# State-space convolution and feed-forward gradients on one core: the magnitudes of the next half block are loaded ahead of the current half block's stores, in a newly laid-out order

## The chip, the cores and the metric

One core of a Trainium2 chip runs the kernel. The metric is the device time of one execution in microseconds (us). Three runs of the kernel before took 584.26, 578.71 and 573.95 us, with a median of 578.71 us. The profile is of one further execution that took 580.12 us.

## The reference

The kernel computes a gated block and all its gradients. The input x (2048 x 512, bf16) is normalised row by row; the normalised rows xn go two ways. One is a long convolution per channel, whose 2048-tap kernel K is made from a diagonal state-space model (512 channels, 128 states each); the other is a feed-forward layer of width 1792. The gate multiplies them.

```python
dt = jnp.exp(log_dt)[:, None]
logdA = dt * (A_re + 1j * A_im)
P = jnp.exp(logdA[:, :, None] * jnp.arange(L)[None, None, :])
K = jnp.einsum("dn,dnl,dn->dl", C_re + 1j * C_im, P, dt * (B_re + 1j * B_im)).real
...
s = irfft(rfft(K padded) * rfft(xn padded))[:L] + xn * Dskip
g = silu(silu(xn @ w1) @ w2)
out = x + s * g
# and the gradients of all inputs for a given grad_out
```

The powers P are what the change concerns. The power exp(logdA * e) has a magnitude exp(dt * A_re * e) and a phase dt * A_im * e. The kernel doesn't make all 2048 of them: it makes 30 per channel and state, and products of these give the rest.

## The kernel before

The 512 channels are worked in four blocks b of 128, and each block in two half blocks h of 64 channels, so there are eight half blocks, (0,0) to (3,1). The work is written as Python generators; each `yield` ends a step. Strings of letters, PLAN, say which generator takes its next step, one letter a step, in seven stages. Each engine (TensorE is PE, VectorE is DVE, ScalarE is ACT, GpSimd is POOL, SyncE is SP, which issues most DMAs) executes its own instructions strictly in the order in which the strings make them, and waits for others by semaphores. SLOTS names the buffer of each tile, and WAYS says for each copy out of PSUM, in the order of its stream, whether ACT (A) or DVE (D) does it. All three were laid out ahead of time by a planner; the kernel only plays them.

Stage 1 (letters F, X, J, P, Q, R, C, U, 9) is where the change lies. In it, `gen_magnitudes` of the setup has already written the 30 magnitudes of all half blocks to Md in DRAM, 128 x 1920 bf16 a half block (480 KB). Then, for each half block:

- P, `gen_phases`: DVE makes the phases V (two tiles, L577 and L580), ACT the sine and cosine sn (L584).
- Q, `gen_powers`: SP loads the magnitudes into one fixed region of the tile ds, columns 5376 to 7296 (L597). DVE multiplies sn by them (L611): one instruction for the first 15 exponents (128x1920) and three for the last 15 (128x640, 128x896, 128x384). They write E, columns 0 to 2688 of ds, the first eighth of Y, and H. SP stores E to Ed (L613). DVE makes the rest of Y in two rounds of three instructions (m1, m2, Y: L622, L624, L626), and SP stores Y to Yd (L628).
- R, `gen_kernel_rows`: DVE multiplies E by the output weights into W (L646), PE contracts W with Y (L652), and after both half blocks of b the rows KE go through DMAs into Kb (L684).
- C, `gen_conv_fwd`: the forward transform of Kb, its product with the spectrum of xn (L477 to L485 on DVE), and the inverse transform.

There is one magnitude region and one E region for all eight half blocks. So the next half block's first multiply needs three things: its magnitudes have landed; the store of the last E has left; all W that read the last E are made. In the kernel before, the load of the magnitudes is the first step of a half block's Q, and so stands on SP behind the Ed and Yd stores of the half block ahead.

X and U are the transforms of xn, F is the feed-forward layer on PE (L764, L781), with J turning its rows. The stages after it hold the backward transforms (D, B), the feed-forward gradients (A, x, w, v) and the gradients of the state-space weights (V, T, S, Z).

Of the kernel before, what the change touches and what calls it, by code (L numbers as in the profile page):

```python
# [24 lines left out]


PLAN = """
2211p22355561566370476p666714575673676601p77167577307777JJ767F85370F7777577p77667763F778677064F88367F7F6FFF8437F67FFFF46
3F66F67FJ67J6F48877F86F68F73/FXXXXJXXFXXFPPFPFQFJPPXFFFPFPFFQFFFFX9QFFPUFFUQXFQXJXFQQQXQPXQXRFFJRPPPRRFXQRFFXPRFQXXRRFPQ
QQFXFFRRFXQQXFFFFFFQQRQFFRFXFUQQQXRRPJPFFXXPRXRFRPFRFXRRFFUPRRFJRRPFRQPRRRRQRQQXXXFXQRRRFQXQQCXRFQPRFQRXPFXFRFQFPFCPRRRU  # L30
FPCCFCCRFCRCQRCCXQFCQQCCPFFCQXQCFRQXFFQQQCCRPFCRCRRCCPFQPXRRRFFCFCFCFRCRRQFXXFRQRXCXQCXQXFFFXRQRCQCQFCRCRRFQCFFRPQCQFFJC
FQPCFRRCXRPRXRPFCCXRXRRPPCPXRCRFUJXXFPXRQXQCQRQPFCFQFXFCQXQRCCQFCFCFCQFFCPCRFFRFFFRFCCFPFCRFCCCQJCCRRRCFRQCCCPRRXCFCCXQC
CXRXQXFQCPRQPFXRJFQCCXRCQPCQRXRCCQFRCCFCRQRQXQRXRRFRFPCFRXPXRUFRCPRFXCCRFFRXFFFQFFXFXRCFQCRCCCCFJFQRXCCQQCFCJFRRQQQRCCCQ
RCCRQRRUCCCRFRRCRCRCRCRRCCRFCRRRRCCR/GGGCFCCGFCGCGFCCFCCGFFFCCCCGCFFCCCCGFLGCCFFGFGGCCCCFFGGFHGFGCCCCCGWCCHFFGHGCFCCGGFC
GCFCCFCCCCGCWFCHCCWCHWWCWHCCWMDHGWCWDGWCWHCCWWWDCDWDDWWGDDWWWWWWDWDLMDWDDMDLCWWLLMDDM/DDDddaDsDDdEaEDADsoaWodBAAABAABADA
DoBADAABDAaBABlDBADABoAADBsDAOBBAAABAOBDaDAABoBABBBABDBDBDBxBBsBADEoxBBBdOoBABOlABxBoxOdoBoxODBAlDBOlOAooxOBaDBBAOEODsxB
DBDDBxOBxaOxDsBBxBBBAOodoBBABADoBoADABBBoBBDBBABDAoBDABdAABDEOAABBxBBAaAABAADDsAooaBBAdBDAAOBBDlBBAOOBlABAAABsDdODDxDDAB
DODoDABODAxADEoDxoOsoAOBDxABBoaBBBAOdxaBOxBoBAABAOoDBOADOABADBDOABxDBBdAxBOBBDBoDxBBsDxEDoBDAoOABBBBaBABBDAABxxDBABABssB
EOOBOBBxBABBxaBBAxBxaABBBBAAaOAABBABBAAOBxBBBAAAAsdAxBBBxBdsBxABBBABBABBABBBsABA/NAYYNNANAYNNVxxddAVAaxYVVAVVYAAVVVYAYVT
AxVVTVATATxVVAATAAAVVVNTxsNTAANAxAVTAATTAVTNSVAVAVYVxNxVYxTYxSYVSTTTYVVATVVxSY/VVTVhVVTVVhttTtVVYTTTSVVYtTVwShtTYVStVVVT  # L40
TVwtTVVwStTtVwTVVZtVVTZtTYVVSSZTTVYVgtwTNNTwYNwgYNVYTShYVvZYVYVvZTVYvVTShYtNVTVtVVTVvvYTwTVtVTgZVVTwSVtVTTvTvSgVtTVvVVtT
TTwVVtTYZVtYhVTVVZVTwwhwVVVZVSTvSNVZTTwZVvTvNYTSNNwYTVtVZtvvtSZtTZYttTvZYYtSVVvhVSTVvVTTTVVVwYYZVTTvtVVVTVTSZTtSwZtTYwVY
VVVwhVVVYSVVSVTVYZTZwtVgVgTTTtwTVVZtZTwvTVYtVZSTZTYVtYShVTVZhwTwSvZZvVYvZZYtVTVvTVZTSTVvtZTvVgTVVVtTTwTgZSTTvSTZvZtZZStS
wZtvZZghvwtZvtZhhZtwwtwZgvZZwZvtZwwZtvv/iitvtkktkwtkvkiimvktwmkkmkvgvmvkmvkwvmkktwvvmkmgkitgwkvvikkmwkkvmmvikvtkvmmvktvg
kwkkwimmvvkmkwvvvkmmvkvvmkvmvkvvvmmvmvm
""".replace("\n", "").split("/")


SLOTS = dict(x.split("=") for x in """
fp.XT=01010101;pf.pf=012012012012012021021020120120121210210210210210210120102102120120121021021021021201201201201201021  # L50
021021021020102102101012012010120210212120101201212102102102102102101021212012010210121210121012012012021021021201202012
0120121012102102102102102;fp.hT=0101010101010101;dft.w8=21301203120131231032102321302310;pc.pc=0101010101010110101010101
010101010101010101010101010101010101010100110101010101010101010101010101010101010101010101010101010101010110101010101010
101011010101010101010101010101010101010101010101010101011010101010101010101010010101010100101001101010101010101010101010
1;fp.ob=0101010;tbl.tv=01011101110101011010101010101010;tbl.ts=01010101010111010010101011010010;tbl.W=010101101011010110
10;dft.t4=010011010101;gate.g=30127456;gate.S=01;da.doT=01010101;da.dhT8=20120120;dftb.w8b=1010;da.dhT6=10101010;go.go_s
=01010101;go.go_r=010101;go.go_g=01010101;go.go_x=01201201;da.pd_s=010101010101;sb.YT=2012012012012012;sb.Eb=01010101;sb
.Gb=01010101;sb.Vb=0101010101010101;sb.Tp=0101010101010101;sb.Sa=1010;fw.h_in=01201201201201;fw.a_tok=10101010101010;fw.
o11=01201201201201;sb.g_acc=0101;fw.dh_tok=0120120;fw.o10=1010101;lw.pd_l=012301;lw.Gt=01230123;lw.m=010101;lw.o1=120312
03  # L60
""".replace("\n", "").split(";") if x)

WAYS = """J=DADAADAA;
F=DDAAAAAAAAADDAAAAAADAAAAAAAAAAAAAAAAAAAAAAADADDAAAAAAAAAAAADDAADDDDADAAA;
X=AAAAAAAAAAAAAAAAAAAAAAAAAAAAAADA;
U=AD;
R=DDAAAAAAAAAAAAAAAAADAADADAADDAAAAAAADDDAAADAAAAA;
C=DDDAAAAAAAAAAAAAAAAADDAAAAAAAADAAAAAADAADAADAADAADDDDDADAAAAAAAA;  # L70
W=ADDDDDDDDDDDDD;
D=AAAADDAAAAAAAAADAAAAAAAAAADAAAAAAAAAAADA;
d=DDDDDAAD;
B=AAAAAAAAAADAAAAAAAAAAAAAAAAAADADADAAAADAAAAAAAAAAAAADADD;
x=ADAADAADAADA;
V=AAAAAAAAAADAAAAADDAAAAAAAAAAAAAAAAADAAADDAAAAAAAAAAAAAAAAAAAAAAA;
Y=DAAAAAAA;
w=AAADAAAAAAAAAA;
v=ADADDADAAAAAADAAAAAAAAAAAAAA"""
# [509 lines left out]
def gen_powers(k, b, h):  # L589

    nc, tbl = k.nc, k.tbl
    TT = nc.vector.tensor_tensor
# [4 lines left out]
    nc.sync.dma_start(tab[:, 5376:5376 + 64 * NX], k.Md[2 * b + h])  # L597
# [4 lines left out]
    k.E[b, h] = E
    for x0 in (0, 15):
        sn = k.sn.pop((b, h, x0))
        if x0 == 0:
            parts = ((E[:, :, :, 1:16, :], 0, 15),)
        else:
            parts = ((E[:, :, :, 16:NE, :], 0, 5), (Y[:, :, :, 1:8, :], 5, 12), (H, 12, 15))
        for o, i0, i1 in parts:
# [1 line left out]
            TT(out=eq(o), in0=qe(sn[:, i0:i1]), in1=qe(m), op=ALU.mult)  # L611
        yield
    nc.sync.dma_start(k.Ed[b, h], tab[:, 0:2688])  # L613
# [4 lines left out]
    out = lambda c: Y[:, c, :, 8:32, :].rearrange("p q (k m) a -> p q k m a", m=8)
    for c, (x, y), op in ((0, ((0, 0), (1, 1)), ALU.subtract), (1, ((0, 1), (1, 0)), ALU.add)):
        m1 = tbl.tile(shp, BF16, name="m1", tag="tv", bufs=2)  # L620
        m2 = tbl.tile(shp, BF16, name="m2", tag="ts", bufs=2)
        TT(out=m1[:], in0=lo(x[0]), in1=hi(x[1]), op=ALU.mult)  # L622
        yield
        TT(out=m2[:], in0=lo(y[0]), in1=hi(y[1]), op=ALU.mult)  # L624
        yield
        TT(out=out(c), in0=m1[:], in1=m2[:], op=op)  # L626
        yield
    nc.sync.dma_start(k.Yd[b, h], Y[:].rearrange("p c q j a -> p (c q j a)"))  # L628
    yield
# [847 lines left out]
```

## Time and profile before

| what | value |
|---|---|
| median of three runs | 578.71 us (573.95 to 584.26) |
| the profiled execution | 580.12 us, span of its instructions 578.3 us |
| PE busy | 527.0 us, 91% of the span |
| DVE busy | 523.8 us, 91% |
| ACT busy | 445.8 us, 77% |
| POOL busy | 77.7 us, 13% |
| moved by DMA | 144.49 MB, 250 GB/s over the span |

The span runs from the first to the last instruction; the 1.8 us between it and the execution's time lie around it. A busy share is an average over stages: PE and DVE have the same share of the span, though not in the same stages. "Idle before" is the time that an engine stood still just ahead of an instruction, and the releaser is what ended it. The chain of waits is followed back from the last instruction, at each step to what released it; a step on it needn't be one that the engine stood still for. Two rows of the page belong to the DMAs that the change moves: the eight loads of magnitudes took 6.8 us each from issue to landing (median), the eight stores of E 6.1 us.

### The profile page before, as it was taken

The numbers are of one execution on the slowest core, as the hardware profiler recorded it, in microseconds if no ns is written. First come the engines' busy times: TensorE is split into PE (matmuls) and PEld (weight loads), VectorE is DVE, ScalarE is ACT, GpSimd is POOL, SyncE is SP. The second block draws the span as 40 slices with busy tenths as digits, with TensorE's granted clock in tenths as the row PEclk, the third lists the DMA queues.
The fourth block names the chain that finished last, engine by engine and source line by source line (L and its number), as shares of the span: only waits on it lengthen the run. The fifth ranks groups of instructions, "written<-read, shape, count | busy, mean of one in ns | idle before, by whom it ended". The sixth has DMA issues, their size and how long they took to land.

```text
span 578.3 us, 14484 instructions
## 1 busy us (share of the span) xinstructions
PE 527.0 (91%) x5982; PEld 395.3 (68%) x6008; DVE 523.8 (91%) x823; ACT 445.8 (77%) x555; POOL 77.7 (13%) x164
## 2 busy tenths in 40 slices
...
GB/s 264 313 276 193 196 281 238 319 260 250 325 225 227 337 287 328 295 254 251 318 261 276 314 249 247 210 208 189 270 231 214 192 272 219 220 199 264 198 204 120
DMA packets 156643, 144.49 MB, mean 250 GB/s; under 512 B 83488, under 2 KB 132896, under 8 KB 153504
## 3 DMA queue, kind: packets, MB, share of 16 engines
...
q0 software_dynamic: 6640, 19.67, 10.1%
...
HBM read 62.78 MB, written 59.25 MB: 211 GB/s over the span
## 4 chain that ended last, share of the span: by engine, by line
PE 41%; DVE 18%; DMA 13%; issue 12%; ACT 9%; POOL 4%; SPq 3%; POOLq 0%; ACTq 0%; DVEq 0%
PE ps_da L1169 8%; PE ps_dx L1193 7%; DMA ds<-Md 6%; PE ps_w L1232 5%; PE ps_i L451 3%; PE ps_v L1021 3%; ACT dA L116 2%; PE ps_w L1261 2%; PE ps_i L464 2%; PE psS L1058 2%; PE pt_t L138 2%; DVE ds L611 2%; DMA YD<-Od 2%; SPq L495 2%; PE ps_s L406 1%
## 5 line engine op out<-in xcount | busy, mean ns | idle before, releaser
L116 ACT CAST dA<-ps_s 128x1024 bf16<-128x1024 f32 x85 | 85.1, 1033 | 9.0 <-PE ps_s L406 6.3
L116 ACT CAST Vb<-ps_v 128x672 bf16<-128x672 f32 x58 | 41.2, 732 | 35.5 <-PE ps_v L1021 23.6
L764 PE MATMUL ps_h<-XT,W 128*128 128x256 bf16 x448 | 57.5, 281 | 10.8 <-DVE XT L117 8.9
L764 PEld LDWEIGHTS <-W 128*128 128x128 bf16 x448 | 43.7, 101 | 19.0 <-issue 11.7
L1169 PE MATMUL ps_da<-doT,W 128*128 128x256 bf16 x448 | 56.2, 273 | 0.0
L1261 PE MATMUL ps_w<-dh_tok,xn 128*128 128x256 bf16 x448 | 52.0, 273 | 2.1 <-ACT o L116 2.0
L116 ACT CAST dB<-ps_i 128x1024 bf16<-128x1024 f32 x42 | 41.6, 1029 | 12.4 <-PE ps_i L451 12.4
L1193 PE MATMUL ps_dx<-W,dhT 128*128 128x512 bf16 x224 | 51.0, 379 | 0.0
L781 PE MATMUL ps_o<-W,aT 128*128 128x512 bf16 x212 | 49.4, 379 | 1.6 <-ACT aT L772 0.6
L1232 PE MATMUL ps_w<-YD,a_tok 128*128 128x512 bf16 x210 | 49.2, 379 | 0.7
L1261 PEld LDWEIGHTS <-xn 128*128 128x128 bf16 x448 | 43.2, 98 | 7.9 <-issue 2.8
L1172 DVE TENSOR_TENSOR dhT<-ps_da,dhT 128x512 bf16<-128x512 f32 x56 | 37.8, 684 | 10.1 <-PE ps_da L1169 9.4
L1169 PEld LDWEIGHTS <-W 128*128 128x128 bf16 x448 | 41.5, 98 | 7.6 <-issue 1.4
L781 PEld LDWEIGHTS <-aT 128*128 128x128 bf16 x224 | 21.1, 98 | 26.2 <-ACT aT L772 2.2
L1193 PEld LDWEIGHTS <-dhT 128*128 128x128 bf16 x224 | 21.1, 98 | 24.2 <-issue 1.2
L1232 PEld LDWEIGHTS <-a_tok 128*128 128x128 bf16 x224 | 21.4, 98 | 23.6 <-ACT a_tok L1223 0.7
L1223 ACT ACTIVATE a_tok<-pt_t 128x1024 bf16<-128x1024 bf16 x28 | 29.1, 1042 | 3.2 <-PE pt_t L138 3.2
L584 ACT ACTIVATE sn<-V 128x1920 bf16<-128x1920 int16 x16 | 29.4, 1835 | 2.5 <-DVE V L580 1.6
L1021 PE MATMUL ps_v<-Gb,YT 128*128 128x168 bf16 x256 | 26.8, 238 | 4.7 <-DMA YT<-Yd 2.2
L1038 DVE TENSOR_TENSOR Tp<-Vb,Eb 128x1344 bf16<-128x1344 bf16 x32 | 27.2, 852 | 3.4 <-ACT Vb L116 3.3
L406 PEld LDWEIGHTS <-TF 128*128 128x128 bf16 x384 | 24.9, 100 | 7.9 <-issue 4.8
L477 DVE TENSOR_TENSOR cm<-sp_in,dA 128x2048 bf16<-128x2048 bf16 x24 | 29.3, 1219 | 0.8
(244 smaller groups left out, 1236.9 us busy)
## 6 DMA issues: line engine op xcount, KB each, us to landing
Yd<-YD SPq DMA_DIRECT2D x8, 1024.0 KB, 6.3
sp_in<-Ud SPq DMA_DIRECT2D x8, 1024.0 KB, 6.3
...
Ed<-ds SPq DMA_DIRECT2D x8, 672.0 KB, 6.1
Eb<-Ed SPq DMA_DIRECT2D x8, 672.0 KB, 4.9
...
KXd<-dA SPq DMA_DIRECT2D x4, 1024.0 KB, 5.7
```

Source lines behind the costliest of these rows:

```text
L116: return self.nc.scalar.copy(out=out, in_=in_)
L406: nc.tensor.matmul(out=ps[:, j], lhsT=k.TF[:, 8 * h + j, c, :], rhs=U(8 * h + j), start=True, stop=True)
L477: TT(out=t2[:], in0=b[:, :, gs], in1=a[:, 1:2, gs].to_broadcast([P, 2, n, P]), op=ALU.mult)
L584: nc.scalar.activation(out=sn[:, 0:n], in_=low, func=ACT.Sin, scale=-2 * PI_LO / 2.0 ** PB)
L764: nc.tensor.matmul(out=ps[:, j], lhsT=k.W1[:, dk, ft * P:ft * P + P], rhs=XTv[:, :, dk, :], start=(dk == 0), stop=(dk == DK - 1))
L781: nc.tensor.matmul(out=ps[:], lhsT=aT[:, ft, t * P:t * P + P], rhs=k.W2[:, ft, :], start=(ft == 0), stop=(ft == FT - 1))
L1021: nc.tensor.matmul(out=ps[:, u, 168 * c:168 * c + 168], lhsT=YT[:, c, q + u, :], rhs=Gb[:, q0 + q + u].rearrange("p w x -> p (w x)"), star ...
L1169: nc.tensor.matmul(out=ps[:, j], lhsT=k.W2[:, ft, dk * P:dk * P + P], rhs=dTv[:, :, dk, :], start=(dk == 0), stop=(dk == DK - 1))
L1172: nc.vector.tensor_tensor(out=dh[:, i0:i0 + 2, :], in0=ps[:], in1=dh[:, i0:i0 + 2, :], op=ALU.mult)
L1193: nc.tensor.matmul(out=ps[:], lhsT=dhs[ft // 8][:, ft % 8, t * P:t * P + P], rhs=k.W1[:, :, ft * P:ft * P + P], start=(ft == 0), stop=(ft ...
L1232: nc.tensor.matmul(out=ps[:], lhsT=at[:, t, :], rhs=k.do[:, t, :], start=(t == 0), stop=(t == k.T - 1))
L1261: nc.tensor.matmul(out=ps[:], lhsT=k.xn[:, t, dk * P:dk * P + P], rhs=dh[:, t].rearrange("p j n -> p (j n)"), start=(t == 0), stop=(t == k ...
```

## The change

`gen_powers` loads the magnitudes itself only for the first half block. For each of the other seven the load is issued by the half block ahead, in a step right behind its last multiply, ahead of its Ed and Yd stores. The load waits on SP for that multiply, since it overwrites what the multiply reads. No load, store or arithmetic instruction is added or taken away.

```diff
     mag = tab[:, 5376:5376 + 64 * NX].rearrange("p (e d) -> p e d", d=64)
-    nc.sync.dma_start(tab[:, 5376:5376 + 64 * NX], k.Md[2 * b + h])
-    yield
+    load = lambda i: nc.sync.dma_start(tab[:, 5376:5376 + 64 * NX], k.Md[i])
+    if (b, h) == (0, 0):
+        load(0)
+        yield
...
             TT(out=eq(o), in0=qe(sn[:, i0:i1]), in1=qe(m), op=ALU.mult)
+        yield
+    if (b, h) != (3, 1):
+        load(2 * b + h + 1)
         yield
     nc.sync.dma_start(k.Ed[b, h], tab[:, 0:2688])
...
-F=DDAAAAAAAAAADDAAAAAADAAAAAAAAAAAAAAAAAAAAAAADADDAAAAAAAAAAAADDAADDDDADAAA;
+F=DADAAAAAAAAADDADAAAAAAAADAAAAAAAAAAAAAAAAAAADADDAAAAAAAAADAADDAADADDADAAA;
...
-R=DDAAAAAAAAAAAAAAAAADAADADAADDAAAAAAADDDAAADAAAAA;
+R=DAAAAAAAAAAAAAAAAAADAADDDADADAAAAAAAADAAAAAAAAAA;
```

PLAN, SLOTS and WAYS are laid out anew for the whole kernel, all seven stages. In WAYS, DVE has 90 copies out of PSUM where it had 96; R gives it 8 for 11, F 16 for 15. Behind the first insertion the lines of the changed kernel are 2 higher, behind the second 5 higher (L611 is L613, L613 is L618, L628 is L633).

The first place is SP's queue from the E store of half block (1,0) to that of (2,0). In it ds<-Md is the load of magnitudes, Ed<-ds the store of E, Yd<-YD the store of Y, Kb<-KE the eight DMAs of the kernel rows of block 0, sp_in<-Ud the load of a spectrum, Ud<-dA and KXd<-dA the stores of spectra. Before:

```order
L613 DMA Ed<-ds 128x2688
L684 DMA Kb<-KE 16x8x256 x8
L628 DMA Yd<-YD 128x4096
L597 DMA ds<-Md 128x1920
L691 DMA sp_in<-Ud 128x4096
L701 DMA Ud<-dA 64x2x2048 x2
L613 DMA Ed<-ds 128x2688
L628 DMA Yd<-YD 128x4096
L597 DMA ds<-Md 128x1920
L715 DMA KXd<-dA 128x4096
L613 DMA Ed<-ds 128x2688
```

And in the changed kernel:

```order
L597 DMA ds<-Md 128x1920
L689 DMA Kb<-KE 16x8x256 x8
L618 DMA Ed<-ds 128x2688
L633 DMA Yd<-YD 128x4096
L706 DMA Ud<-dA 64x2x2048 x2
L696 DMA sp_in<-Ud 128x4096
L597 DMA ds<-Md 128x1920
L618 DMA Ed<-ds 128x2688
L633 DMA Yd<-YD 128x4096
L720 DMA KXd<-dA 128x4096
L597 DMA ds<-Md 128x1920
L618 DMA Ed<-ds 128x2688
```

The load has moved from behind Yd to ahead of Ed. The store of E of (1,0) now stands behind the eight Kb DMAs as well, where it stood ahead of them.

The second place is DVE from the last multiply of half block (0,1) to the first of (1,0), W<-ds,CT being the reads of E, m and YD the making of Y, V the phases. Before, its last rows are:

```order
L626 TENSOR_TENSOR YD<-m_970,m_971 128x16x96
L646 TENSOR_TENSOR W<-ds,CT 128x1344 x2
L577 TENSOR_TENSOR V<-tau,ecst 128x15x64
L580 TENSOR_SCALAR V<-V 128x15x64
L646 TENSOR_TENSOR W<-ds,CT 128x1344 x2
L117 COPY TI<-pt_i 128x2048
L577 TENSOR_TENSOR V<-tau,ecst 128x15x64
L580 TENSOR_SCALAR V<-V 128x15x64
L611 TENSOR_TENSOR ds<-sn,ds 128x15x32x4
```

And in the changed kernel:

```order
L631 TENSOR_TENSOR YD<-m_1002,m_1003 128x16x96
L651 TENSOR_TENSOR W<-ds,CT 128x1344
L577 TENSOR_TENSOR V<-tau,ecst 128x15x64
L580 TENSOR_SCALAR V<-V 128x15x64
L651 TENSOR_TENSOR W<-ds,CT 128x1344 x2
L577 TENSOR_TENSOR V<-tau,ecst 128x15x64
L613 TENSOR_TENSOR ds<-sn,ds 128x15x32x4
```

The copy TI and one L580 that stood ahead of the multiply now stand behind it, and one copy hT and one W among the rows of Y ahead; the multiply has less DVE work between it and the one before.

The third place is SP around the stores of half blocks (2,1) and (3,0), Sd<-S_b being the store of a convolution's output. In the changed kernel:

```order
L730 DMA Sd<-S_b 128x2048
L597 DMA ds<-Md 128x1920
L706 DMA Ud<-dA 64x2x2048 x2
L696 DMA sp_in<-Ud 128x4096
L618 DMA Ed<-ds 128x2688
L633 DMA Yd<-YD 128x4096
L720 DMA KXd<-dA 128x4096
L597 DMA ds<-Md 128x1920
```

Before, the spectrum load, the two Ud stores and the Sd store came in that order ahead of Ed, Yd and the load. Now the load waits for (2,1)'s multiply ahead of the Ud stores and of that spectrum load.

More of the change, by code (lines that the diff above doesn't have):

```diff
@@ L32 @@
[L32 to L45, printed above, removed]
+22123515255p676p41674560J777577673J77077776757p71737607775p71777F87776FF3F6F7F867706168F644760F663666786F487373636667F3F
@@ new lines @@
+6F7366F5878F8FF6F67478/XJFXJFPFFFFXXQXJXJFFXFXFPFPPFFPFPFFFX9FPFFFQUQFXQPFQFQQUFFRXQQXPQRXXFFQXRXQPXFXFFRRFPPFRRFFFXPFFR
+XXFFPQQQQFQRXQFFRFURQQXJFRXFXQFRQPFRXFRJXFPRPRQPXRRFFFRRJRRPJQRFFRFPQPRXRFRRRQURRRQQQXQFXFQFXXXQRQXRPCRXFFRPXFRPPFRRQFPC
+CFCFCFCCXRQQRCRCUQQFFCRCCRFCCPQQCFXFRXFCQQQPQFCRCRCCQRCXRCRPFRCRPRFXXCFXFQCQRFXFRQFXCQFQFRCRRCQCFPCQFQFXRRCQPCFXFRRRFJQF
+FRCCCRFQCPFCCRXFPRXXXPJRPCXCFPRRXCRPXQFQCFXQFCRPXPUQFRFQQXCFXQRCCRFFCFRRCFQCCFFQFFFFPQCQFCCRFCFRCJCCFRCCRCRCCRRCCQCPCXQX
+FCPXFXCXXJQRFQQRFPRQFXCCXRCQPRQCRCRRCRQCCFCFRFRXFRQCRPXRURFRPCXRRFQPFCRXFFFXXQQFRXCFFCCFCXQQRFFCQQCCFFRCCQCCFQRCCRQRCXJQ
@@ new lines @@
+CRRJCRRCCRURRCCRCRCFRCRCCRRCCCCRFRRRRC/FCCGFGCCFCFGCCFGCFFCFGCCGGGGFCFCLCCCCGFFFGCCGCGFCGCFFHFGGCCCCWGGGCCFHFGCHCCFGGCFC
+CFCGGFCCCCGCCWHCFCCWWCWHCHWCCWWDWCHDGCWHCCWWCWDWDWDDMWWWDWGWWWDWDWDDLMCDWLMDLLWWDMDDMDD/DdDadDWsEDdDAdBAaoBAAaAADBoDasAD
+AEBDAAABBADlBABDAADABABDBosDAAAoBABOADoABBDBoABBBBAAsDBOBBDoDDEBBBaxxBABOBABlOxdBolOOBooBxoDBxAxBaADEOBBOsBBDBADdOxABlDB
+xBoDBxDxOalODBBBAsBxAaBoBBABDdDBBBBBBBAABdBBDDAoOAADBBoAAAAEBDaoOABBAooOdDBsOABDOAAABOABBAdDAABxDBBABDBODDBAAOxDDsABDDoD
+xExOADoBADAosxBDOBoABxDoAOBABAoABABBBxOOBlaAAAoDBOADDOBOBoBoBxDBBxOsDABBaDDBBDBxAEoOxsDxxBABDAAaBOABBodAdBBAaBDoxBOAODxB
@@ new lines @@
+BABBBBxBBOOEBBOABBxAaBaABBBsOAxABxAABBBABABBBBAAAAdAsBBsxBBBdBBdABAdBxBBAABBBBBA/NANNYsNNYAxAYANxVAaYAVVVAxAYxYVVVVYVAAV
+ATTVATVAVVAsVTxATxVVTVAAATATSASNATNxATANNVVVAVxVNAVATYVVATYxTYxxYYTSVVTVxVAVS/YVVTTVVTTSTVVVhtTtTtVVhSttTwYtVVVtwtYwVVVw
+TVVVVVTSTTYSThYVTtVTVVwYwVtZTtSTgtgZYVZwZYNTTVNvTTVvNVTvSYYYvhYvVNTVtVVTShTwvVSVtVVTYYvVgTTVtNgVVYVtTSTwVVtvSTVtVZTZwVVV
+ZtTtVTTZVVwTwwTZVVvSVTTNYwhTSZZZVNSTVNYZVZNVvVTvTtZZttTYhvVYVvTtYtvtSVtYZSYTVtVVvwVvTVYVVhwZVvTSTTTVYVTVTwVVYgwSYTVSTTtV
+VwTtVTVVYVYwVhSStTVtTVVgTVVZwTTwTTVZZZtVVVYvTZSttZYVYwTSTZVvZTtvhVSVSwgZYZYvZvVVVTZTvVZVVVTTZZTVtTTwTtTSwTtSTgZTvZtvhStw
@@ L46 @@
+ZvgSvhZvttZwtZvwZtZZZvwvhZtZgZZZ/tikvtwtkvitgkvwvvkkmvkvmtvkivhviktwvgwkkvimmkwkkmvvikvmmvvtwgkkkmkmmvkvwtvkkwiktmmktkwk
+vgmikmwmvkmkkmvkvwvmvvvmwvkmkmmvmvvvmvv
 """.replace("\n", "").split("/")
 SLOTS = dict(x.split("=") for x in """
[L50 to L52 removed]
@@ L53 @@
[L53 to L57, printed above, removed]
+fp.XT=01010101;pf.pf=012010210210210210201201201201210201201201201201201021021021012012012010210210210120120120120120210
@@ new lines @@
+210210210212010120120120120201202102102102102102102102102102102012012012102102102102101021012021021201021021012012120120
+2102102012021021021021021;fp.hT=0101010101010101;fp.ob=0101010;dft.w8=21031230123102302103213032013201;pc.pc=01010101010
+100010101010101010101010101010101010101010101010101010101101010101010101010101010101010101010101010101010101010101010101
+010101010101010101010101010101010101001011010101010101010101010101010101011010101010101010101110101010101010010101010101
+010101010101010;tbl.tv=01011010001010100101001011101010;tbl.ts=01010101010111011101010111010010;tbl.W=010101101011010110
@@ L58 @@
+10;dft.t4=010100101010;gate.S=01;gate.g=10672345;da.doT=01010101;da.dhT8=20120120;dftb.w8b=1010;da.dhT6=10101010;go.go_s
+=01010101;go.go_r=010101;go.go_g=01010101;go.go_x=01201201;da.pd_s=010101010101;sb.YT=0120120120120120;sb.Eb=10101010;sb
 .Gb=01010101;sb.Vb=0101010101010101;sb.Tp=0101010101010101;sb.Sa=1010;fw.h_in=01201201201201;fw.a_tok=10101010101010;fw.
-o11=01201201201201;sb.g_acc=0101;fw.dh_tok=0120120;fw.o10=1010101;lw.pd_l=012301;lw.Gt=01230123;lw.m=010101;lw.o1=120312
-03
+o11=01201201201201;sb.g_acc=0101;fw.dh_tok=0120120;fw.o10=1010101;lw.pd_l=012301;lw.Gt=01230123;lw.m=010101;lw.o1=123012
```

25 lines of the change are left out of this document (11 added, 14 removed).

## The prediction

> **What bounds the kernel now.** I read the page's busy times first, then busy time by stretch, then the waits on the moved DMA, then the chain of waits.
>
> ```profile
> span 578.3 us, 14484 instructions
> PE 527.0 (91%) x5982; PEld 395.3 (68%) x6008; DVE 523.8 (91%) x823; ACT 445.8 (77%) x555; POOL 77.7 (13%) x164
> ```
>
> Two engines have the same share, so the stretches must say which one sets the pace where. Columns are stretch, length, busy time of PE, weight loads, DVE, ACT and POOL, granted clock, DMA share, GB/s:
>
> ```profile
> 0.00:50.00 50.00, 26.31 (x185) 18.87 (x187) 45.04 (x110) 40.32 (x57) 19.92 (x69) 0.97 0.84 260
> 50.00:100.00 50.00, 45.11 (x513) 33.61 (x515) 47.66 (x67) 46.68 (x56) 5.82 (x8) 1.00 0.87 244
> 100.00:150.00 50.00, 47.94 (x616) 35.98 (x619) 49.26 (x65) 49.65 (x59) 4.61 (x6) 1.00 0.91 275
> 150.00:205.00 55.00, 51.68 (x712) 39.55 (x715) 51.20 (x66) 48.58 (x58) 4.58 (x6) 1.00 0.88 283
> 205.00:378.00 173.00, 170.63 (x2166) 126.20 (x2165) 161.55 (x211) 143.66 (x150) 11.42 (x20) 1.00 0.87 273
> 378.00:503.00 125.00, 119.63 (x1230) 91.55 (x1236) 112.26 (x173) 78.77 (x115) 13.30 (x24) 0.99 1.02 219
> 503.00:571.00 68.00, 65.61 (x572) 49.52 (x575) 56.84 (x138) 37.72 (x64) 17.50 (x32) 1.00 0.87 222
> ```
>
> Up to 205 us, the setup and stage 1 where the powers are made, DVE is the fullest engine: it stands still 5.0, 2.3, 0.7 and 3.8 us in the first four rows, 11.8 us in all. In 50 to 205 alone DVE lacks 6.9 us, PE 10.3 and ACT 10.1, so all three are nearly full. From 205 us on PE is the bound: it lacks 2.4, 5.4 and 2.4 us in the last three rows, 10.1 us of 366. Whatever stage 1 saves or loses moves the moment when PE gets its uninterrupted run, and little else.
>
> Now the load that is moved. The row of waits (us in total, times, longest), the row of the chain of waits by line, and the chain's four pieces on this load (start, length):
>
> ```profile
> DVE ds L611 <- DMA ds<-Md: 3.4, 2, 1.9
> PE ps_da L1169 8%; PE ps_dx L1193 7%; DMA ds<-Md 6%; PE ps_w L1232 5%; PE ps_i L451 3%; PE ps_v L1021 3%; ACT dA L116 2%; PE ps_w L1261 2%; PE ps_i L464 2%; PE psS L1058 2%; PE pt_t L138 2%; DVE ds L611 2%; DMA YD<-Od 2%; SPq L495 2%; PE ps_s L406 1%
> 75.51 9.26 DMA ds<-Md
> 95.04 7.68 DMA ds<-Md
> 151.20 10.57 DMA ds<-Md
> 176.57 5.57 DMA ds<-Md
> ```
>
> These differ by ten: the chain carries the load for 9.26 + 7.68 + 10.57 + 5.57 = 33.1 us, but DVE stood still for it 3.4 us, in two of eight cases. The timeline shows both, in its last bracket:
>
> ```profile
> 84.87 1.56 DVE L611 TENSOR_TENSOR ds<-sn,ds 128x1920 bf16<-128x1920 bf16 x2 [1.93 <-DMA ds<-Md]
> 161.86 1.16 DVE L611 TENSOR_TENSOR ds<-sn,ds 128x1920 bf16<-128x1920 bf16 x1 [1.52 <-DMA ds<-Md]
> ```
>
> In the other 30 us DVE was doing other work that has to be done anyway. So 3.4 us is the price of the late load, not 33.
>
> **The change, part by part.** *The load moves ahead of two stores.* SP's queue around half block (0,1) shows by how much:
>
> ```profile
> 68.56 1.23 SPq L613 DMA_DIRECT2D Ed<-ds  x1
> 75.07 0.34 SPq L628 DMA_DIRECT2D Yd<-YD  x1
> 75.51 0.82 SPq L597 DMA_DIRECT2D ds<-Md  x1
> 88.86 5.50 SPq L684 DMA_DIRECT2D Kb<-KE  x8
> ```
>
> The load will go where the E store went, 75.51 - 68.56 = 7.0 us earlier. Both waits, 1.93 and 1.52 us, are shorter than that, and are covered if the load lands as it does now. Nothing is added: the same eight loads, eight E stores and eight Y stores. Gain on DVE: 3.4 us; bounds 0 (it waits for something else at the same moment) and 6.9 us (all that DVE lacks in 50 to 205, if the planner used the freedom for more).
>
> *The E store moves behind the load.* This is the new wait to fear. The next first multiply overwrites E, so it waits for the store, and behind it on DVE stands all of stage 1. Sizes and landing times, then smallest, median and largest time to landing of the load and of the E store:
>
> ```profile
> Yd<-YD SPq DMA_DIRECT2D x8, 1024.0 KB, 6.3
> Ed<-ds SPq DMA_DIRECT2D x8, 672.0 KB, 6.1
> ds<-Md SPq DMA_DIRECT2D x8, 480.0 KB, 6.8
> DMA to landing us min/median/max: 4.2/6.8/10.6
> DMA to landing us min/median/max: 3.0/6.1/8.7
> ```
>
> Before, the load is issued 0.4 us behind a Y store of 1024 KB (75.07, 75.51) and still lands in 6.8 us. So standing behind 480 KB shouldn't cost the E store more than those 480 KB at the rate of the rows above, 244 to 283 GB/s, or 1.7 to 2.0 us. I take 0.8 (the load's issue, the longer form above) + 6.1 + 2.0 = 8.9 us from the last multiply to the landing of E; the upper end is both in line at the load's largest, 0.8 + 10.6 + 6.1 = 17.5 us.
>
> The Trainium skill, page "DMA: Bandwidth & Descriptors", section "Queues, rings and completion order", says that on each DMA engine descriptors are consumed in ring order and that SP owns one ring on each, so E's data would follow the load's. Where the 0.4 us row above puts a load behind a larger store, the trace doesn't contradict it; by it the landing stays at the 8.9 us taken, as the 2.0 us are already in.
>
> Against it stands the DVE work between a last multiply and the next first one, from these groups (last numbers: busy us, mean ns of one, idle ahead):
>
> ```profile
> L622 DVE TENSOR_TENSOR m<-YD,ds 128x1536 bf16<-128x1536 bf16 x16 | 15.2, 952 | 0.2
> L624 DVE TENSOR_TENSOR m<-YD,ds 128x1536 bf16<-128x1536 bf16 x16 | 15.4, 963 | 0.0
> L626 DVE TENSOR_TENSOR YD<-m,m 128x1536 bf16<-128x1536 bf16 x16 | 15.2, 952 | 0.2
> L646 DVE TENSOR_TENSOR W<-ds,CT 128x1344 bf16<-128x1344 bf16 x32 | 26.4, 855 | 0.0
> L577 DVE TENSOR_TENSOR V<-tau,ecst 128x960 int32<-128x960 f32 x16 | 18.4, 1147 | 0.0
> L580 DVE TENSOR_SCALAR V<-V 128x960 int32<-128x960 int32 x16 | 11.1, 692 | 0.2
> L117 DVE CAST hT<-ps_h 128x512 bf16<-128x512 f32 x14 | 9.5, 682 | 2.4 <-PE ps_h L764 2.2
> L117 DVE CAST ds<-ps_k 128x336 bf16<-128x336 f32 x10 | 5.0, 496 | 0.9 <-PE ps_k L652 0.9
> ```
>
> From (0,1) to (1,0), the order's shortest: two rounds of m, m, Y (2 x 2.867), hT (0.682), four W (4 x 0.855), two L577 (2.294), one L580 (0.692), 12.8 us by means, about 11.9 after the 0.06 us or so by which neighbours overlap. Summed likewise, the seven distances are 13.0, 11.9, 16.5, 12.6, 19.9, 15.8 and 18.9 us; before they were 14.1, 13.1, 15.4, 13.8, 19.7, 17.0 and 17.6. All exceed 8.9. The third is special: its E store stands behind eight Kb issues, 5.50 us, and 8.9 + 5.5 = 14.4 is still under 16.5. Cost taken: 0; at the upper end, 17.5 us, the seven fall short by 4.5, 5.6, 6.5 (with the Kb issues), 4.9, 0, 1.7 and 0, or 23.2 us.
>
> *The spectrum load behind (2,1)'s multiply.* The Ud stores and one sp_in now wait for that multiply. Its spectrum is used on DVE some 14 us of work later (m, V, W, copies and the two rounds of Y, by the same means), and the DMA's kind lands in 6.3 us (the Yd row, of the same 1024 KB): 0, at worst what the E store costs there.
>
> *The new order.* It has the same instructions but for the engine of some copies: six fewer on DVE in the whole kernel, three of them the ps_k copies of 0.496 us, 1.5 us less in stage 1, and one hT copy of 0.682 more there. I take 0 of it for the path: ACT lacks as much as PE there. In the sums of DVE's work up to its landmarks (first multiplies, W, phases, products) the two orders agree within 1 to 3 us all along, by the mean durations of their groups; so do the sums of PE's. Bounds for what it does elsewhere: the three runs of one and the same order lie 5 us either side of their median, so I take 0 with 5 each way.
>
> The sum: DVE gains 3.4 us; PE and ACT lack about 10 us each in 50 to 205, so they can follow, but not in every place; I pass on 2 of the 3.4, between 0 and all. 580.12 - 2 = 578.1 us against the profiled execution, which is 1.4 us above the median of the runs; against the median 576.7. I say 577.5 us, between the two.
>
> **The rivals.** *The load is no earlier in effect.* SP is in order: the load for (3,0) stands behind an Sd store that waits for ACT, that for (1,1) behind two transposing DMAs. For it: SP issues are spread over 5.50 us where they wait for slots. Against: both places where DVE waited need only 2 us of the 7. Then the 3.4 us stay: 578.7 us.
>
> *The E store takes the place of the load.* The mechanism above: DVE's first multiply of each half block waits for E to leave. It costs from a landing 11.9 us behind the last multiply, and decides (over 15 us lost, against 3.4 won) from a landing of about 16 us in the usual half block. At 17.5 us: 580.1 - 3.4 + 23.2 - 1.4 = 598.5 us. For it: DMAs are 87 to 91% busy there, and loads have taken 10.6 us. Against: E's largest was 8.7 us.
>
> *The new order opens gaps on PE after 205 us.* PE lacks only 10.1 us of 366 there; an order that fits less well more than doubles it, plus 12 us: 591 us. Against: its landmarks hardly move.
>
> *The powers were the pace.* If the 33.1 us of chain really held stage 1, the gain would be all that DVE lacks up to 205 us, 11.8 us: 580.1 - 11.8 - 1.4 = 566.9 us. Against: DVE's 99% busy in 100 to 150; 5.0 of these 11.8 us lie in the first 50 us, where the load plays no part.
>
> **How the numbers follow.** A measurement of this kernel tells about 2% from no change, so faster is below 567.1 and slower above 590.3 us. The forecast has 0.52, the load no earlier 0.14, the E store 0.12, gaps on PE 0.14 (0.10 of them over 2%), the powers as the pace 0.08. That gives faster 0.08, same 0.70, slower 0.22. The likeliest case's own range is 572 to 584 us; to leave out no more than 2 in 10, the range reaches to 568 and, into the slower cases, to 592 us.
>
> **What would show it.** Right: no row of DVE L613 waiting for DMA ds<-Md; the load gone from the chain of waits or nearly so; the E store landing within 9 us; DVE still the fullest up to 205 us; PE at 97% or more after. Wrong: a row of DVE waiting on Ed<-ds or of DVE's own queue ahead of L613; stage 1 ending past 205 us; PE lacking over 20 us behind it.

## The result and the profile after

The changed kernel takes 573.97 us (median; 569.93 to 576.86) against 577.98 us for the kernel before on the same chip: a ratio of 0.9928 [0.9903, 0.9953]. Two repeats beside the later experiments gave 0.9888 [0.9847, 0.993] and 0.994 [0.9906, 0.9975]. So it is 0.6 to 1.1% faster. That is less than the 2% which count as a change of this kernel: the same, as forecast, inside 568 to 592, and 3.5 us below the 577.5 us said. Medians are of all executions and ratios leave out the few that ran in a slower state, so a ratio isn't exactly the quotient of two medians.

The page after, its span, busy times and the chain of waits by line:

```profile
span 571.7 us, 14504 instructions
...
PE 526.4 (92%) x5983; PEld 395.3 (69%) x6008; DVE 520.0 (91%) x817; ACT 446.6 (78%) x561; POOL 75.7 (13%) x164
...
PE ps_dx L1198 7%; PE ps_da L1174 7%; PE ps_w L1237 5%; PE ps_w L1266 4%; PE ps_o L786 3%; PE ps_i L451 3%; PE ps_h L769 3%; ACT dA L116 3%; PE ps_i L464 3%; ACT mag_all L518 3%; PE pt_t L138 2%; PE ps_s L406 2%; DMA Ed<-ds 2%; ACT dB L116 2%; DMA dh_tok<-DHd 2%
```

The load, 6% of the chain before, is gone from this row of the fifteen largest; of its 33.1 us one piece of 4.2 is left. `DMA Ed<-ds` is now in the row at 2%, one piece of 12.4 us; before, the chain had one of 6.4. The waits of VectorE on its multiplies, all of them:

```profile
DVE ds L613 <- DMA Ed<-ds: 1.8, 1, 1.8
```

No wait is left on the load (3.4 us before), and one of 1.8 us is new, on the E store; in two later profiles of the same changed kernel it is 0.2 us and none. The busy time by stretch, in the prediction's columns:

```profile
0.00:50.00 50.00, 29.55 (x215) 21.41 (x218) 47.01 (x121) 43.40 (x60) 18.94 (x69) 0.90 0.96 270
50.00:100.00 50.00, 45.57 (x549) 34.41 (x550) 48.14 (x61) 47.60 (x58) 5.90 (x8) 1.00 0.88 260
100.00:150.00 50.00, 49.38 (x623) 37.19 (x623) 49.86 (x67) 49.77 (x58) 4.67 (x7) 1.00 0.90 269
150.00:205.00 55.00, 52.31 (x723) 38.70 (x726) 52.18 (x63) 46.02 (x58) 5.00 (x8) 1.00 0.91 287
205.00:378.00 173.00, 168.48 (x2109) 125.38 (x2105) 155.57 (x202) 145.62 (x151) 9.95 (x18) 0.99 0.87 269
378.00:503.00 125.00, 122.14 (x1283) 94.89 (x1290) 117.57 (x187) 80.68 (x123) 13.28 (x24) 1.00 1.04 227
503.00:571.00 68.00, 58.92 (x500) 43.35 (x503) 49.68 (x120) 33.48 (x57) 17.99 (x32) 0.97 0.84 206
```

TensorE has about as much work in all as before (526.4 and 527.0 us), so the difference of its busy time, row by row, says where it gets ahead: 3.2 us in the first 50 us, 0.5, 1.4 and 0.6 in the next three rows, -2.2 in 205 to 378, and 2.5 in 378 to 503. So most comes ahead of 50 us, where no load of the loop has yet been waited for, and behind 205 us part is given back. The 2.5 us of 378 to 503 can't be told from the spread: those two later profiles of the changed kernel have 123.03 and 119.54 us of TensorE there, for 122.14 here.

Three landmarks of the timeline, before and after: the first multiply of half block (0,0), SP's first issue of the last block's kernel rows Kb (the end of stage 1's powers), and TensorE's first use of those rows. Before:

```profile
50.27 1.15 DVE L611 TENSOR_TENSOR ds<-sn,ds 128x1920 bf16<-128x1920 bf16 x1
...
204.62 5.41 SPq L684 DMA_DIRECT2D Kb<-KE  x4
...
215.45 1.05 PE L406 MATMUL ps_s<-Kb,TF 128*128 128x128 bf16 x16 [0.31 <-DVE hT L117]
```

After:

```profile
47.76 1.55 DVE L613 TENSOR_TENSOR ds<-sn,ds 128x1920 bf16<-128x1920 bf16 x2
...
199.00 7.94 SPq L689 DMA_DIRECT2D Kb<-KE  x4
...
212.09 1.86 PE L406 MATMUL ps_s<-Kb,TF 128*128 128x128 bf16 x16 [2.30 <-issue]
```

The lead is 2.5 us at the first multiply, 5.6 at the first Kb issue and 3.4 at Kb's first use. So the start gave 2.5, stage 1 gave 3.1 more, and 2.2 were lost again between the issue of Kb and its use. Each is read off one execution of each kernel. The two later profiles of the changed kernel have the landmarks at 47.73, 195.70 and 209.96 us and at 47.52, 198.07 and 212.01, so the sign of each step repeats, but behind the first multiply its size is good to 2 or 3 us only. The profiled execution before was also 2.1 us above its kernel's median (580.12 against 577.98).

The end of the start, by the busy time of 40 to 50 us, before and then after:

```profile
40.00:50.00 10.00, 8.53 (x74) 7.44 (x74) 9.36 (x14) 6.79 (x7) 2.10 (x5) 0.83 0.50 120
```

```profile
40.00:50.00 10.00, 9.15 (x99) 7.93 (x98) 9.78 (x20) 9.97 (x11) 1.47 (x2) 1.00 0.83 196
```

ScalarE worked 6.79 of these 10 us before and works 9.97 now. VectorE, the fullest engine here, works 47.01 of the first 50 us where it worked 45.04: the new order leaves it standing 2.0 us less there. Which of the moved steps did that wasn't tested.

### The profile page after: what moved, and what is told of

It reads as the page before. It is cut to its first block, busy times and chain, and to the rows that moved or that the text cites. A ratio compares the mean times of both kernels' runs of the same rounds, so it can differ in the third digit from the quotient of the medians.

```text
span 571.7 us, 14504 instructions
## 1 busy us (share of the span) xinstructions
PE 526.4 (92%) x5983; PEld 395.3 (69%) x6008; DVE 520.0 (91%) x817; ACT 446.6 (78%) x561; POOL 75.7 (13%) x164
## 4 chain that ended last, share of the span: by engine, by line
PE 48%; DVE 17%; ACT 14%; issue 9%; DMA 8%; SPq 2%; POOL 1%; POOLq 0%; ACTq 0%; DVEq 0%
PE ps_dx L1198 7%; PE ps_da L1174 7%; PE ps_w L1237 5%; PE ps_w L1266 4%; PE ps_o L786 3%; PE ps_i L451 3%; PE ps_h L769 3%; ACT dA L116 3%; PE ps_i L464 3%; ACT mag_all L518 3%; PE pt_t L138 2%; PE ps_s L406 2%; DMA Ed<-ds 2%; ACT dB L116 2%; DMA dh_tok<-DHd 2%
## 5 line engine op out<-in xcount | busy, mean ns | idle before, releaser
L116 ACT CAST dA<-ps_s 128x1024 bf16<-128x1024 f32 x82 | 82.2, 1035 | 7.3 <-PE ps_s L406 5.1
L769 PE MATMUL ps_h<-XT,W 128*128 128x256 bf16 x448 | 59.5, 286 | 9.3 <-ACT hT L116 8.4
L479 DVE TENSOR_TENSOR sp_in<-sp_in,dA 128x2048 bf16<-128x2048 bf16 x24 | 29.3, 1222 | 0.6
L451 PE MATMUL ps_i<-I,sp_in 64*128 64x128 bf16 x768 | 27.2, 217 | 2.6 <-ACT KE L116 1.4
```

The lines of the kernel that those rows point to most:

```text
L116: return self.nc.scalar.copy(out=out, in_=in_)
L451: nc.tensor.matmul(out=ps[:, z, g], lhsT=Y[zs, c, g0 + g, :], rhs=k.I2[zs, c].rearrange("p c m -> p (c m)"), start=(c == 0), stop=(c == 1))
L479: TT(out=b[:, :, gs], in0=b[:, :, gs], in1=a[:, 0:1, gs].to_broadcast([P, 2, n, P]), op=ALU.mult)
L769: nc.tensor.matmul(out=ps[:, j], lhsT=k.W1[:, dk, ft * P:ft * P + P], rhs=XTv[:, :, dk, :], start=(dk == 0), stop=(dk == DK - 1))
```

## The experiments

The question was which of the change's two parts, the load's place and the new order, made the 4 us; then what the store behind the load can cost; then where the gain behind stage 1 went. Kernels were compared with the kernel before on the same chip.

**Early load in the old order.** In the kernel before, the load of the next half block is issued right ahead of the E store, in the same step.

```
-    nc.sync.dma_start(tab[:, 5376:5376 + 64 * NX], k.Md[2 * b + h])
+    load = lambda i: nc.sync.dma_start(tab[:, 5376:5376 + 64 * NX], k.Md[i])
+    if (b, h) == (0, 0):
+        load(0)
...
+    if (b, h) != (3, 1):
+        load(2 * b + h + 1)
     nc.sync.dma_start(k.Ed[b, h], tab[:, 0:2688])
```

> The order of before, with one thing moved: each load of magnitudes but the first is issued directly ahead of the E store, about 7 us earlier on SP; nothing else changes its place on any engine. If the late load is what the change gained from (theory 1): DVE's 3.4 us of waiting on ds<-Md go, stage 1 ends about 3 us earlier, 575 us, ratio 0.995. If the gain came from the new order alone (theory 2): DVE finds another wait or PE keeps the pace, 578 us, ratio 1.000. If the E store behind the load hurts (theory 3): waits on Ed<-ds of several us, 580 us or more.

577.16 us, 0.9984 [0.9948, 1.0019]: not told from no change, nor from the 0.995 of theory 1. VectorE no longer waits for the load, and the same landmarks read:

```profile
51.39 1.15 DVE L613 TENSOR_TENSOR ds<-sn,ds 128x1920 bf16<-128x1920 bf16 x1
...
204.60 4.78 SPq L688 DMA_DIRECT2D Kb<-KE  x4
...
214.95 1.06 PE L406 MATMUL ps_s<-Kb,TF 128*128 128x128 bf16 x16
```

From the first multiply to the first Kb issue it took 153.2 us (204.60 - 51.39), where before took 154.4 (204.62 - 50.27). So of the 3.4 us of waiting about 1.1 came through in these two profiles, and the time moved by 0.8 us, within its interval.

**New order with the late load.** In the changed kernel the load goes back behind the Y store.

```
     if (b, h) != (3, 1):
-        load(2 * b + h + 1)
         yield
...
     nc.sync.dma_start(k.Yd[b, h], Y[:].rearrange("p c q j a -> p (c q j a)"))
+    if (b, h) != (3, 1):
+        load(2 * b + h + 1)
     yield
```

> The changed kernel's order, with the load put back behind the Y store, where it was before. The new order's first multiplies come 1 us of DVE work sooner after the last than in before, so if the load matters (theory 1) DVE waits for ds<-Md at least the 3.4 us of before, rather 5 to 8 us, and the time is 578 to 581 us, ratio 1.000 to 1.005. If the gain is the order's alone (theory 2): 574 us, ratio 0.993.

589.15 us, 1.0184 [1.0131, 1.0237]: slower than before, well past the 578 to 581 us expected. The waits on the multiplies, then SP's queue and the multiply behind the longest of them:

```profile
DVE ds L613 <- DMA ds<-Md: 8.7, 5, 3.2
...
DVE ds L613 <- issue: 7.8, 1, 7.8
```

```profile
175.14 5.67 SPq L690 DMA_DIRECT2D Kb<-KE  x8
180.92 0.53 SPq L697 DMA_DIRECT2D sp_in<-Ud  x1
181.55 0.37 SPq L632 DMA_DIRECT2D Yd<-YD  x1
181.97 0.42 SPq L597 DMA_DIRECT2D ds<-Md  x1
```

```profile
193.06 1.56 DVE L613 TENSOR_TENSOR ds<-sn,ds 128x1920 bf16<-128x1920 bf16 x2 [7.83 <-issue]
```

The wait that the view puts down to "issue" ends 11.1 us behind that load's issue (193.06 - 181.97), and this very load took 11.0 us to land, so it is the load too: 16.5 us of waiting in six places, where the old order had 3.4 in two. The first multiply is at 47.55 us, as early as with the whole change (47.76), so the start is the new order's and not the load's. Together: the load alone -0.8 us, the order alone +11.2, both -4.0. They don't add up: the new order brings the next multiply closer and is good only with the early load, while the old order had work laid in that already covered the late one. In the longest of these waits the place on SP adds to it: the new order puts the eight Kb issues, 5.67 us, ahead of that load, where before the load stood ahead of them (176.57 and 177.04 us).

**Store right behind the load, and store ahead of the load.** In the first, the E store is issued in the load's step, directly behind it; in the second, directly ahead of it.

```
     if (b, h) != (3, 1):
         load(2 * b + h + 1)
-        yield
-    nc.sync.dma_start(k.Ed[b, h], tab[:, 0:2688])
+        nc.sync.dma_start(k.Ed[b, h], tab[:, 0:2688])
+        yield
+    else:
+        nc.sync.dma_start(k.Ed[b, h], tab[:, 0:2688])
     yield
```

```
+    nc.sync.dma_start(k.Ed[b, h], tab[:, 0:2688])
     if (b, h) != (3, 1):
         load(2 * b + h + 1)
         yield
-    nc.sync.dma_start(k.Ed[b, h], tab[:, 0:2688])
```

> The changed kernel with the E store issued right behind the load, never behind Kb, Ud or sp_in DMAs. The changed kernel's one DVE wait on Ed<-ds, 1.8 us at half block (3,0), goes if it came from standing behind the Ud stores and the spectrum load (theory: place on SP): 572 to 573 us, ratio 0.990. If it came from standing behind the load itself or from full DMA engines, it stays: 574 us, 0.993.

> As the one before, but the E store ahead of the load, both in one step. If the E store is held up by the load's 480 KB, E lands about 2 us sooner and the load about 2 us later than with the load ahead; both still inside 11.9 us of DVE work, so the time is the same as there, within 1 us (572 to 574 us). If ring order decides more than that, E's median landing goes from 7.4 us to 5 us and the load's from 4.2 to 7.

574.08 us, 0.9924 [0.9887, 0.9962], and 575.61 us, 0.9944 [0.9913, 0.9974]: neither is told from the changed kernel, though no wait on a multiply exceeds 0.5 us. The second is 1.6 us above the 572 to 574 expected. The wait of 1.8 us is 0.3 in the first; as the changed kernel's repeats have 0.2 and none, that isn't told from their spread. Both issue Kb earlier (197.42 and 196.09 us) than the changed kernel's 199.00, but not earlier than its repeats' 195.70. The second, at the last two landmarks:

```profile
196.09 9.52 SPq L689 DMA_DIRECT2D Kb<-KE  x4
...
212.07 1.86 PE L406 MATMUL ps_s<-Kb,TF 128*128 128x128 bf16 x16 [5.02 <-DMA Kb<-KE]
```

Kb is issued 2.9 us earlier than in the changed kernel's first profile and used at the same moment (212.07, 212.09), after a wait of 5.0 us. What stage 1 gains there waits for these eight transfers.

**E store late.** The E store goes behind the Y store; the load stays early.

```
-    nc.sync.dma_start(k.Ed[b, h], tab[:, 0:2688])
     yield
...
     nc.sync.dma_start(k.Yd[b, h], Y[:].rearrange("p c q j a -> p (c q j a)"))
+    nc.sync.dma_start(k.Ed[b, h], tab[:, 0:2688])
     yield
```

> The changed kernel, but the E store of each half block is issued behind its Y store instead of ahead of the powers' arithmetic; the load stays early. It sizes the rival that the E store can take the load's place. The two are about 7 us apart on SP (68.56 and 75.07 us around half block (0,1) before), and the changed kernel's E store lands 7.4 us after its issue (median, largest 12.4), so it should land about 14.4 us behind the last multiply, 19 at worst, against 11.9 to 19.9 us of DVE's work up to the next first multiply. Theory (the distance from last to first multiply is the cover, and 7.4 us fits in it while 14.4 does not): DVE waits for DMA Ed<-ds in four to six of the seven half blocks, 8 to 14 us in all, and the time is 580 to 588 us. Rival (the E store is never on the path, since other work of DVE's can go first): no such rows beyond 2 us, and 573 to 576 us.

586.64 us, 1.0118 [1.008, 1.0157]. The rival of the E store, made real:

```profile
DVE ds L613 <- issue: 9.2, 1, 9.2
...
DVE ds L613 <- DMA Ed<-ds: 7.3, 5, 2.1
```

```profile
175.74 5.74 SPq L689 DMA_DIRECT2D Kb<-KE  x8
181.59 0.53 SPq L696 DMA_DIRECT2D sp_in<-Ud  x1
182.22 0.37 SPq L632 DMA_DIRECT2D Yd<-YD  x1
182.64 0.42 SPq L633 DMA_DIRECT2D Ed<-ds  x1
```

VectorE stands 16.5 us in six places, above the 8 to 14 expected; the time is 13.2 us above the changed kernel's 573.41 us of the same comparison. The longest is again behind the eight Kb issues: the multiply starts at 195.25 us, 12.6 us after the store's issue at 182.64, and this store took 12.5 us to land.

**KX store late.** To free the way for Kb, block 2's KX store (1024 KB, ahead of Kb on SP) is issued at the end of that block's convolution: once in the changed kernel, once with the E store ahead of the load.

```
-    nc.sync.dma_start(k.KXd[b], KX[:].rearrange("p c g k -> p (c g k)"))
+    if b != 2:
+        nc.sync.dma_start(k.KXd[b], KX[:].rearrange("p c g k -> p (c g k)"))
...
+    if b == 2:
+        nc.sync.dma_start(k.KXd[b], KX[:].rearrange("p c g k -> p (c g k)"))
     (nc.scalar if b == 3 else nc.sync).dma_start(k.Sd[b], S[:].rearrange("p t d -> p (t d)"))
```

> The changed kernel, but the store of the spectrum KX of block 2 (1024 KB on SP at 196.49 us, right ahead of the last block's eight Kb issues) is issued at the end of that block's convolution, beside the store of S. It asks where the rest of the gain went: the changed kernel issues the first Kb of block 3 at 199.00 us, 5.6 us ahead of before (204.62), but PE takes Kb up at 212.09, only 3.4 ahead of 215.45, after waits of 2.3 and 2.2 us. Theory (those Kb transfers have become the wait, held up by the KX store ahead of them): PE takes Kb up at 208 to 210.5 us, its waits there fall by 2 us or more, and the time is 570 to 572.5 us against 574. Rival (the DMA engines are full of other transfers there as well, or PE has other work to do first): the same first use within 1 us of 212, and 573 to 575 us.

> As the run before, but with the E store right ahead of the load in one step, which ended stage 1 earliest (first Kb of block 3 at 196.09 us) and then waited longest for Kb (5.0 us at one place, first use at 212.07 us). Theory (Kb's transfers hold it up): first use at 206 to 209 us and 568.5 to 572 us in all, the fastest version. Rival (other transfers fill the DMA engines there): first use stays at 211 to 213 us and the time at 574 to 576 us, as without the late KX store.

Both missed: 584.01 us, 1.0079 [1.0045, 1.0113], and 582.66 us, 1.0055 [1.002, 1.009]. The first one's timeline:

```profile
196.54 5.12 SPq L689 DMA_DIRECT2D Kb<-KE  x4
...
206.90 1.06 PE L406 MATMUL ps_s<-Kb,TF 128*128 128x128 bf16 x16
...
220.15 1.01 ACT L116 CAST dA<-ps_s 128x1024 bf16<-128x1024 f32 x1 [12.90 <-DMA KXd<-dA]
```

The first half of the theory held in this run: Kb is used at 206.90 us, 10.4 us behind its issue instead of 13.1. In the second it didn't: issued at 196.31 and used at 209.27, 13.0 us. And in both the convolution that starts there copies its result into the tile that KX occupies, and a store issued 10 us later holds that tile 10 us longer: 12.9 us of waiting. I hadn't asked who needs the tile next.

**KX store by another queue, or right behind Kb.** The store is issued by GpSimd at its own place, in the changed kernel and in the one with the E store first; and in the changed kernel on SP, behind the last Kb issue.

```
-    nc.sync.dma_start(k.KXd[b], KX[:].rearrange("p c g k -> p (c g k)"))
+    (nc.gpsimd if b == 2 else nc.sync).dma_start(k.KXd[b], KX[:].rearrange("p c g k -> p (c g k)"))
```

```
+        if b == 3 and i == 7:
+            nc.sync.dma_start(k.KXd[2], k.KX2[:].rearrange("p c g k -> p (c g k)"))
...
-    nc.sync.dma_start(k.KXd[b], KX[:].rearrange("p c g k -> p (c g k)"))
+    if b == 2:
+        k.KX2 = KX
+    else:
+        nc.sync.dma_start(k.KXd[b], KX[:].rearrange("p c g k -> p (c g k)"))
```

> The changed kernel, with the store of block 2's KX issued at its own place, but by GpSimd instead of SP. The late store has shown two things: without it ahead of them Kb's SP issues took 5.12 us instead of 7.94 and 7.54, and PE took Kb up at 206.90 instead of 212.09 and 209.96 us; but the store then kept KX's tile until 220 us, and ScalarE and VectorE stood 12.9 and 12.4 us for it. Here the store leaves at its old time. Theory Q (Kb was held up behind the store on SP's queue): Kb's SP issues take about 5 us, PE takes Kb up at 206 to 208.5 us, nothing waits on KXd, and the time is 569 to 572 us. Theory B (it was the store's 1024 KB on the DMA engines, about 4 us at 250 to 270 GB/s, whatever the queue): first use stays at 210 to 212 us and the time at 573 to 575 us.

> The E store right ahead of the load in one step, as in the fourth run, with block 2's KX store issued by GpSimd. That order ended stage 1 earliest (first Kb issue at 196.09 us) and lost it again at Kb (first use at 212.07). By theory Q first use is at 205 to 208 us and the time 568 to 571.5 us, the fastest version; by theory B first use stays at 210 to 212 us and the time at 574 to 576 us.

> The changed kernel, with the store of block 2's KX on SP right behind the last of the eight Kb issues of block 3: about 202 us instead of 196.49, and 4 us ahead of the late store (206.33 to 209.14). Theory (what the late store lost was the time for which KX's tile was held): PE takes Kb up at 207 us as there, the waits for KXd fall from 12.9 and 12.4 to 5 to 8 us, and the time is 576 to 580 us. Rival (the late store lost by its bytes among the YD and Gr loads): 572 to 575 us, with no wait for KXd over 2 us.

572.25 us, 0.988 [0.985, 0.991]; 572.61 us, 0.9883 [0.9845, 0.9922]; 575.12 us, 0.9898 [0.9867, 0.993]. The changed kernel beside them had 575.64 us, 0.994 [0.9906, 0.9975]. The first two are 3 us below it by their medians. But the changed kernel's own three ratios run from 0.9888 to 0.994, so none is shown to be faster than the change. With the other queue, in the changed kernel and then with the E store first:

```profile
199.25 6.44 SPq L689 DMA_DIRECT2D Kb<-KE  x4
...
211.25 1.06 PE L406 MATMUL ps_s<-Kb,TF 128*128 128x128 bf16 x16
```

```profile
195.54 8.76 SPq L689 DMA_DIRECT2D Kb<-KE  x4
...
209.32 1.05 PE L406 MATMUL ps_s<-Kb,TF 128*128 128x128 bf16 x16 [2.80 <-issue]
```

From issue to use these are 12.0 and 13.8 us, against 13.1 in the changed kernel, 14.3 and 13.9 in its repeats, and 10.4 and 13.0 with the late store. The second run lies between the two theories, in its first use (209.32) and its time. So it wasn't the queue, or not chiefly, and not the store alone. Right behind Kb it is 12.7 us (195.90 to 208.59), with 5.1 us of ScalarE on the held tile, as expected, though the time came out below the 576 to 580.

SP's own waits on these issues say more than either theory. In the changed kernel, then before:

```profile
SPq L689 <- DMA sp_in<-Ud: 3.1, 1, 3.1
SPq L689 <- DMA Kb<-KE: 2.1, 1, 2.1
```

```profile
SPq L684 <- DMA KXd<-dA: 2.1, 1, 2.1
```

SP holds an issue back until an earlier transfer has landed: the spectrum load, the KX store, or the first of the Kb themselves. In the trace each held issue waits for the same semaphore that its own transfer then counts up, so I read it as waiting for a free semaphore and not for data. The last Kb is thus issued 7.4 us behind the first in the changed kernel (206.39 - 199.00), 4.9 before (209.48 - 204.62). By then GpSimd has issued loads of grad_out, 512 KB each:

```profile
204.10 1.09 POOL L807 DMA_DIRECT2D Gr<-in_grad_out_dram  x2
```

Two things hold in all fourteen profiles of this document. The first Kb lands 0.2 to 0.6 us behind the landing of the KX store or of the spectrum load ahead of it, whichever is later, and by whichever queue the store went; with the store out of the way the spectrum load takes its place. And the last Kb takes 5.3 to 7.4 us to land in the nine profiles where it is issued behind a grad_out load, and 2.8 to 4.3 us in the other five. The two runs with the late store fall on both sides: issued at 201.11 ahead of that load at 201.31, and at 201.67 behind it at 201.16. This is read off the traces; no run moved the grad_out loads or freed the held issue.

**The changed kernel again**, once beside each of the last two groups:

> The changed kernel as it is, for comparison with these on one chip: 572 to 576 us, a ratio of 0.990 to 0.995 by every theory.

> The changed kernel as it is, for comparison on the same chip: 572 to 576 us, ratio 0.987 to 0.995.

573.41 and 575.64 us, with the ratios given above.

## Why the prediction was right, and where its steps were not

*DVE is the fullest up to 205 us, TensorE behind:* right. After the change VectorE lacks 3.0, 1.9, 0.1 and 2.8 us in the first four rows, 7.8 for 11.8. TensorE has 97% and 98% in 205 to 503, though 87% in the last row, whose end comes closer to the span's end now. So the rival of new gaps on TensorE didn't come either: it lacks 7.4 us in those two rows, and lacked 7.7.

A range of 24 us would have held a forecast of no change as well, so it is the steps that tell whether the reasoning was right.

*3.4 us, not 33, is what the late load cost:* right. Taking it away where nothing else moves brought 1.1 us of stage 1 and 0.8 us of time with an interval of 2 us each way, in line with the 2 of 3.4 passed on, and against the 11.8 us of the rival on the powers' pace. The interval doesn't tell 0.8 us from nothing, so how much of the 3.4 is passed on stays open. A DMA can stand in the chain for 33 us while the engine behind it works.

*The load has 7 us to spare, and lands as before:* right in its result, since no wait is left. Two readings on the way were off. The load shown behind a Y store (75.51) took 9.3 us to land, not the median 6.8. And the eight SP issues of 5.50 us, given as waiting for slots, follow each other at about 0.6 us each.

*The E store lands 8.9 us behind the last multiply:* too high for four of the seven half blocks, too low for three. Landing times of load and E store after the change:

```profile
DMA to landing us min/median/max: 3.8/4.2/8.7
```

```profile
DMA to landing us min/median/max: 5.4/7.4/12.4
```

With an issue 0.4 us behind the multiply (50.52 for the first) that is 7.8 us by the median landing. In (1,1) the landing alone took 9.9 us, 10.3 in all; in (1,0), behind the eight Kb issues, it came 15.9 us behind the multiply, where the prediction had 14.4. Both were covered. Half block (2,1) wasn't:

```profile
138.84 0.32 SPq L597 DMA_DIRECT2D ds<-Md  x1
139.25 2.10 SPq L706 DMA_DIRECT2D Ud<-dA  x2
141.45 2.06 SPq L696 DMA_DIRECT2D sp_in<-Ud  x1
143.57 2.02 SPq L618 DMA_DIRECT2D Ed<-ds  x1
...
156.08 1.16 DVE L613 TENSOR_TENSOR ds<-sn,ds 128x1920 bf16<-128x1920 bf16 x1 [1.80 <-DMA Ed<-ds]
```

Its E store is issued 4.8 us after the last multiply's end (138.8), behind two Ud stores and a spectrum load, and lands at 156.0: 17.2 us, the upper end of the prediction's 17.5. Its cover of 15.8 us fell short by 1.8, where the prediction's list has 1.7 for such a landing. The step on the spectrum load behind that multiply asked only who waits for the spectrum; it should have asked which DMA stands behind it.

Of the rule of the Trainium skill, page "DMA: Bandwidth & Descriptors", section "Queues, rings and completion order" (descriptors of a ring are consumed in order), the runs show this: with the store right behind, the load lands in 4.8 us and the store in 7.1; with the store right ahead, the load in 6.4 and the store in 5.8. What stands behind lands later, as the rule would have it: by 1.3 us for the store and 1.6 for the load, by the medians. For the store that is less than the 1.7 to 2.0 us that the prediction took for the 480 KB ahead.

*The E store's cover suffices, so its move costs 0:* nearly. The row of VectorE waiting on `Ed<-ds`, named as a sign of being wrong, is there, at 1.8 us in one place; in the repeats it is 0.2 us and none, so it is at the edge of its cover. The runs also priced the rival: a store 7 us later costs 16.5 us of waiting and 13 us of time.

*The new order, taken as 0 with 5 either way:* the term that was mis-sized. It gave 2.5 us ahead of the first multiply, and with the early load 2.0 more in stage 1 than the old order got out of the same load (151.2 us from the first multiply to Kb for 153.2; 148.0 and 150.6 in the repeats). So most of the 4.0 us came from a term that the sum had at 0. That the time stayed inside the range is owed to the 5 us allowed for that term, not to the sum. The sums over landmarks, equal within 1 to 3 us, were too coarse for that, and blind to the other side: they count work, not what has landed, so they could not show that the new order loses 11 us with the late load.

*From stage 1's end everything moves along:* only in part. Of 5.6 us at the issue of Kb 3.4 were left at its use. From issue to use TensorE does the same 10.5 us of work before and after, by busy time in these two stretches:

```profile
204.60:215.40 10.80, 10.49 (x142) 7.72 (x140) 8.42 (x11) 5.58 (x8) 2.63 (x5) 1.00 0.89 256
```

```profile
199.00:212.00 13.00, 10.53 (x141) 7.80 (x140) 8.31 (x10) 6.16 (x9) 3.55 (x7) 1.00 0.87 279
```

Before, that work covered Kb but for 0.3 us; now Kb takes 13 us and TensorE stands for the rest. The longer way is that of the held issues: 7.4 us from the first to the last where it was 4.9. What holds them, the spectrum load and the KX store, lands 8.8 and 9.6 us behind its issue for 5.8 and 7.4 before. Why these two land later in the new order stays open.
